# Two layers of cached attention and an MLP on one core: half a MB of the first wq and half a MB of the last w2 moved to partitions 0 to 31

## The chip, the core and the metric

The kernel runs on one core of a Trainium2 chip. TensorE (PE in the profile, with its weight loads as PEld) multiplies, VectorE (DVE), ScalarE (ACT) and GpSimd (POOL) do the rest, and SyncE (SP) issues nearly all the DMAs. The core has 16 DMA engines, which move data from HBM into SBUF, a memory of 128 partitions. The metric is the device time of one execution in microseconds (us), as the median of several runs.

## The reference

One token of each of 8 sequences passes through two identical layers, with the same weights both times. All data are float32.

```
B, D = 8, 1024;  Hq, Hkv, Sk, Dh = 32, 4, 4096, 128;  F = 3584
for layer in range(2):
    x = x + attention(layernorm(x) @ wq, k_cache, v_cache) @ wo
    x = x + gelu(layernorm(x) @ w1 + b1) @ w2 + b2
```

Here wq is 1024 x 4096 and wo 4096 x 1024 (16 MB each), w1 is 1024 x 3584 and w2 3584 x 1024 (14 MB each), and each of the 8 sequences has 8 MB of keys and 8 MB of values. One layer reads some 188 MB; the second layer finds a little of the cache still in SBUF.

## The kernel before, in words

**The arena.** One SBUF tile, `arena`, holds all that is streamed. It has 216 units of 256 columns (1 KB in each partition, so 128 KB in a unit). Three large slots A, B and C begin at units 0, 64 and 128, and four small ring slots R of 8 units at 184, 192, 200 and 208. Small intermediates have places of their own in the ring's units: the spread-out queries (`AT_QZ`, 3 units), a row of scores (`AT_ROW` or `AT_ROW2`, 4 units) and the turned probabilities (`AT_S`, 4 units).

**The stream.** `weights` and `cache` (lines 414 to 432) write one list, `stream`, with every load of both layers in the order in which it will be used: a name, a place and the piece of DRAM. `pump` (line 160) takes loads from its head while their places are free, and issues each as one DMA on SP's queue. `give` frees a place and pumps again, so a load is issued when the work that read the old contents is through. Since SP issues in order, a load that waits holds all the later ones back. The large loads are issued long before they are used; the ring of 8 unit slots, which carries wo, w1, w2 and wq between the two layers, runs four loads ahead.

**The rows of a load.** A load writes 128 rows, one in each partition: 64 KB each for a load of 8 MB, 4 KB each for one of 512 KB.

**The products.** `expand` (line 174) multiplies the normalised row by wq or w1, in two halves u of 8 contraction blocks; with wq, one half is 8 MB. `project` (line 262) multiplies by wo or w2 and adds to the row: each contraction block of 128 rows is 4 units (512 KB), and takes four matmuls that write four groups of 32 output partitions. The first `expand` waits for the input row, the first half of wq, and then the second half. The last `project`, `p1`, reads w2 in six pieces of 40, 28, 20, 12, 8 and 4 units; after it come one addition on VectorE and the store of the result.

**Attention.** For each sequence `scores` multiplies the queries by the keys, `probs` and `turn` make and transpose the probabilities, `values` multiplies by the values, and `heads` scales the result. In layer 0 the order of the loads is K0, V0 up to K7, V7, then wo (`o0`). The first three pieces of `o0` have free ring slots before the attention ends; the fourth goes where `AT_S` lies, and waits until the last values are through.

**Small loads.** The bias b2 is loaded by four DMAs of 8 rows of 1 KB (line 475), queued behind K0, and b1 by one DMA of 128 rows of 112 bytes behind them.

Of the kernel before, what the change touches and what calls it, by code (L numbers as in the profile page):

```python
# [8 lines left out]
F32 = mybir.dt.float32  # L9
# [5 lines left out]
P = 128  # L15
B, D = 8, 1024
# [20 lines left out]
SLOT = 64  # L37
AT_A, AT_B, AT_C, RING = 0, 64, 128, 184
N_KB = 216
AT_QZ, AT_ROW, AT_S, AT_ROW2 = 200, 208, 212, 203  # L40
Q_AT = (0, 48, 72, 32)
QW = 88
DMA_SCRATCH = 512
# [3 lines left out]
def decode_layers(ctx: ExitStack, tc: tile.TileContext, x, kc, vc, wq, wo, w1, b1, w2, b2, out):  # L47
# [82 lines left out]
    def layernorm(xr, rsum):  # L130
# [23 lines left out]
        pending.append(variance)  # L154
        return rs

    stream = []
    held = {}

    def pump():  # L160
        while stream and is_free(stream[0][1], stream[0][2]):
            key, at, n, src = stream.pop(0)
            take(at, n, key)
            nc.sync.dma_start(out=arena[:, at * KB:at * KB + src.shape[1]], in_=src)
            held[key] = at, n

    def loads(name):
        i = 0
# [2 lines left out]
            yield i, at, n  # L171
            i += 1

    def expand(name, unit, rs, finish, hooks={}):
        heights = [(unit // P - j + 3) // 4 * P for j in range(4)]
        for u in range(2):
            acc = ps_o.tile([P, CH], F32, tag="o", name="acc")
            at = 0
            begun = set()
            end = NT * unit  # L180
            for i, base, n_kb in loads((name, u)):
                c = given = 0
                cols = min(n_kb * KB, end - at)
                while c < cols:
                    kt, a = divmod(at, unit)
                    n = min(unit - a, cols - c)
                    blocks = arena[:, base * KB + c:base * KB + c + n].rearrange("p (t q) -> p t q", q=P)
                    t0, t1 = a // P, (a + n) // P
                    for j in range(4):
                        ts = range(t0 + (j - t0) % 4, t1, 4)  # L190
                        if len(ts):
                            r = ts[0] // 4
                            nc.tensor.matmul(acc[32 * j:32 * j + 32, r * P:(r + len(ts)) * P],  # L193
                                             xnT[:, kt * B:kt * B + 32],
                                             blocks[:, ts[0] - t0:ts[-1] - t0 + 1:4],
                                             start=(j not in begun), stop=(kt == NT - 1 and ts[-1] + 4 >= unit // P))
                            begun.add(j)
# [64 lines left out]
    def project(name, n_k, lhs, rsum, hooks={}):  # L262
        y = ps_o.tile([P, CH], F32, tag="o", name="y")
        kt = 0
        step = D // KB
        for i, base, n_kb in loads(name):
            for c in range(0, n_kb, step):
                for j in range(4):
                    e = (base + c) * KB + j * Q4
                    nc.tensor.matmul(y[32 * j:32 * j + 32, 0:Q4], lhs[:, kt * B:kt * B + 32], arena[:, e:e + Q4],  # L270
                                     start=(kt == 0), stop=(kt == n_k - 1))
                kt += 1
                if kt in hooks:
                    hooks[kt]()
                if c + step == n_kb:
                    give(base, n_kb)
                if kt >= 4:
                    flush()
        assert kt == n_k
        nc.vector.scalar_tensor_tensor(x_row, y[:, 0:Q4], 1.0, x_row, op0=ALU.mult, op1=ALU.add, accum_out=rsum)  # L280
# [133 lines left out]
    def weights(name, dram, parts):  # L414

        for u in range(dram.shape[0]):
            a = 0
            for i, (at, n) in enumerate(parts[u]):
                cols = min(n * KB, dram.shape[2] - a)
                stream.append((((name, u) if dram.shape[0] > 1 else name, i), at, n, dram[u, :, a:a + cols]))  # L420
                a += cols
            assert a == dram.shape[2]

    def cache(layer, keys, dram, parts):

# [76 lines left out]
    for layer in range(2):  # L502
        pieces.update({key: at for (e, key), at in places.items() if e == layer})
        rs = layernorm(x_row, rsum)
        if layer == 0:
            expand("q0", W, rs, query_unit)
            flush()
            last = attention(range(B), kept, after={6: park})
        else:
# [10 lines left out]
        project(f"p{layer}", NFT, hT, rsum)  # L520

    nc.sync.dma_start(out=out, in_=x_row)

# [52 lines left out]
```

## Time and profile before

| | |
|---|---|
| time, median of 3 runs | 872.83 us (872.7 to 873.04) |
| the profiled execution | 873.06 us, span 871.1 us |
| TensorE busy | 535.9 us, 62% of the span, 4056 matmul instructions and as many weight loads |
| VectorE, ScalarE busy | 181.9 us and 47.5 us |
| HBM read | 369.28 MB, 424 GB/s over the span |
| queue q1 (SP's loads) | 17056 packets, 99.1% of the time of 16 DMA engines |
| queue q8 (blocks of TensorE's instructions) | 31 packets of 16 KB, 0.2% |

The span is what the profile sees of an execution; the execution's own time is 1.96 us longer. The profile has no column for a single DMA engine. It gives the share of time in which the 16 were busy, and for a stretch of time the number of packets of each queue. A packet here is one row of a load (or the 4 byte write that reports a load's end on one engine). The packed trace behind the profile holds each packet's start, length, size and queue, but not the engine it ran on.

### The profile page before, as it was taken

The page shows a single profiled execution, that of the slowest core. Times are in us where ns is not written, and L with a number is a line of the kernel's source. Part 1 is how long each engine was busy: PE and PEld are TensorE (multiplying, and loading weights), DVE is VectorE, ACT ScalarE, POOL GpSimd, SP SyncE. Part 2 cuts the span into 40 slices and gives each one's busy share as a digit, 9 for nine tenths or more (in the row PEclk, how much of TensorE's full clock was granted, in tenths as well). Part 3 has the DMA queues.
Part 4 walks back from the last instruction along what each step waited for, and adds up shares of the span by engine and source line. Part 5 has one row for each costly group of instructions (what it writes and reads, how often), then busy time and mean ns, then how long its engine had stood idle before and what let it go on. Part 6 is the DMA issues. An engine that isn't in the chain of part 4 may idle for free.

```text
span 871.1 us, 9135 instructions
## 1 busy us (share of the span) xinstructions
PE 535.9 (62%) x4056; PEld 179.3 (21%) x4056; DVE 181.9 (21%) x587; ACT 47.5 (5%) x75; POOL 2.6 (0%) x14
## 2 busy tenths in 40 slices
PE   0547566655667566776667766766565655665565
PEld 0112121211212122222222122222121211222222
DVE  0001221313122232200100034332232313120110
ACT  0200000000000010000000010000000000000000
POOL 0000000000000000000000000000000000000000
PEclk9877777877777778868876799987787777777889
DMA  9999999999999999999999999999999999999997
GB/s 390 434 433 434 434 431 434 433 431 434 436 428 434 436 412 428 400 420 420 421 421 418 418 426 438 440 431 431 433 431 431 433 434 433 432 433 440 419 423 296
DMA packets 17239, 369.99 MB, mean 425 GB/s; under 512 B 2064, under 2 KB 2352, under 8 KB 3504
## 3 DMA queue, kind: packets, MB, share of 16 engines
q1 hardware_dynamic: 17056, 369.28, 99.1%
q8 instruction: 31, 0.51, 0.2%
q10 hardware_dynamic: 144, 0.13, 0.0%
q14 instruction: 8, 0.07, 0.0%
HBM read 369.28 MB, written 0.13 MB: 424 GB/s over the span
## 4 chain that ended last, share of the span: by engine, by line
DMA 72%; PE 21%; DVE 5%; issue 1%; ACT 1%; SPq 0%; ACTq 0%; DVEq 0%
DMA arena<-in_A_v_cache_dram 27%; DMA arena<-in_B_w_dram 17%; DMA arena<-in_A_k_cache_dram 16%; PE sps L303 6%; PE o_ps L360 6%; DMA arena<-in_A_wo_dram 6%; DMA arena<-in_A_wq_dram 4%; PE acc L193 3%; DVE scratch L368 3%; DMA x_row<-in_A_x_dram 3%; PE y L270 2%; PE sps L375 1%; DVE scratch L366 1%; PE s_ps L303 1%; DVE arena L311 1%
## 5 line engine op out<-in xcount | busy, mean ns | idle before, releaser
L303 PE MATMUL sps<-arena 128*32 128x512 f32 x944 | 135.4, 712 | 90.3 <-DMA arena<-in_A_k_cache_dram 78.1
L360 PE MATMUL o_ps<-arena 128*32 128x512 f32 x1024 | 154.7, 732 | 8.4 <-DMA arena<-in_A_v_cache_dram 8.3
L270 PE MATMUL y<-arena,oT 128*32 128x256 f32 x960 | 79.3, 476 | 50.3 <-DMA arena<-in_A_wo_dram 28.5
L193 PE MATMUL acc<-arena,xnT 128*32 128x512 f32 (+3 forms) x608 | 78.5, 618 | 47.7 <-DMA arena<-in_B_w_dram 27.2
L368 DVE SCALAR_TENSOR_TENSOR scratch<-o_ps,misc,scratch 128x128 f32<-128x128 f32 x192 | 67.3, 351 | 6.8
L303 PEld LDWEIGHTS sps<-arena 128*32 128x32 f32 x944 | 30.0, 125 | 173.2 <-DMA arena<-in_A_k_cache_dram 77.0
L338 PE MATMUL sps<-ident,arena 128*128 128x128 f32 x128 | 30.2, 379 | 43.6 <-ACT arena L327 31.7
L270 PEld LDWEIGHTS y<-arena,oT 128*32 128x32 f32 x960 | 32.2, 130 | 97.5 <-DMA arena<-in_A_wo_dram 33.2
L375 PE MATMUL sps<-misc,scratch 128*128 128x8 f32 x128 | 27.5, 287 | 33.4 <-DVE scratch L368 33.4
L311 DVE TENSOR_SCALAR_CACHE_REDUCE arena<-sps 128x512 f32<-128x512 f32 x30 | 20.8, 692 | 121.6 <-PE sps L303 121.6
L327 ACT ACTIVATE arena<-arena,bias 128x1024 f32<-128x1024 f32 x16 | 18.4, 1148 | 506.4 <-DVE scratch L324 506.4
L360 PEld LDWEIGHTS o_ps<-arena 128*32 128x32 f32 x1024 | 30.9, 127 | 69.5 <-issue 58.3
L375 PEld LDWEIGHTS sps<-misc,scratch 128*128 128x128 f32 x128 | 21.6, 212 | 104.9 <-DVE scratch L368 85.7
L366 DVE TENSOR_SCALAR scratch<-o_ps,misc 128x128 f32<-128x128 f32 x64 | 22.5, 351 | 95.8 <-PE o_ps L360 95.8
L193 PEld LDWEIGHTS acc<-arena,xnT 128*32 128x32 f32 x608 | 20.4, 122 | 93.1 <-DMA arena<-in_A_wq_dram 36.8
L377 DVE TENSOR_TENSOR oT<-sps,scratch 128x8 f32<-128x8 f32 x64 | 11.1, 173 | 113.6 <-PE sps L375 113.6
L338 PEld LDWEIGHTS sps<-ident,arena 128*128 128x128 f32 x128 | 19.2, 186 | 52.1 <-ACT arena L327 35.5
L280 DVE SCALAR_TENSOR_TENSOR x_row<-y,x_row 128x256 f32<-128x256 f32 x4 | 1.7, 424 | 104.8 <-PE y L270 104.8
L320 PE MATMUL sps<-scratch,misc 128*128 128x128 f32 x32 | 7.8, 326 | 18.7 <-DVE scratch L316 18.7
L343 DVE COPY arena<-sps 128x512 f32<-128x512 f32 x16 | 11.1, 692 | 38.5 <-PE sps L338 38.5
L345 PE MATMUL sps<-scratch,misc 128*128 128x32 f32 x32 | 10.0, 404 | 12.5 <-DVE arena L343 12.5
L132 PE MATMUL sps<-nmean,rsum 128*128 128x64 f32 x8 | 2.0, 336 | 25.3 <-DVE rsum L473 23.6
(74 smaller groups left out, 134.5 us busy)
## 6 DMA issues: line engine op xcount, KB each, us to landing
arena<-in_B_w_dram SPq DMA_DIRECT2D x27, 1024.0 KB, 8.6
arena<-in_A_wo_dram SPq DMA_DIRECT2D x15, 1024.0 KB, 8.0
arena<-in_A_wq_dram SPq DMA_DIRECT2D x15, 1024.0 KB, 8.3
arena<-in_B_w_dram SPq DMA_DIRECT2D x2, 7168.0 KB, 45.2
arena<-in_A_k_cache_dram SPq DMA_DIRECT2D x3, 4096.0 KB, 19.5
arena<-in_A_v_cache_dram SPq DMA_DIRECT2D x3, 4096.0 KB, 22.5
arena<-in_A_v_cache_dram SPq DMA_DIRECT2D x4, 2048.0 KB, 18.2
arena<-in_B_w_dram SPq DMA_DIRECT2D x1, 5120.0 KB
```

What stands on the lines that cost most here:

```text
L193: nc.tensor.matmul(acc[32 * j:32 * j + 32, r * P:(r + len(ts)) * P], xnT[:, kt * B:kt * B + 32], blocks[:, ts[0] - t0:ts[-1] - t0 + 1:4], ...
L270: nc.tensor.matmul(y[32 * j:32 * j + 32, 0:Q4], lhs[:, kt * B:kt * B + 32], arena[:, e:e + Q4], start=(kt == 0), stop=(kt == n_k - 1))
L303: nc.tensor.matmul(ps[32 * g:32 * g + 32, :], q[:, c:c + 32], kt[:, g * CH:(g + 1) * CH], start=(j == 0), stop=(j == HKV - 1))
L311: nc.vector.tensor_scalar(row[:, half * CH:(half + 1) * CH], ps, SCALE, None, op0=ALU.mult, op1=ALU.max, accum_out=st["mx"][:, half:half + 1])
L327: nc.scalar.activation(row, row, AF.Exp, bias=bias, scale=1.0, accum_out=ls)
L338: nc.tensor.transpose(pp[:, t * P:(t + 1) * P], row[:, c:c + P], ident)
L343: nc.vector.tensor_copy(s[:, half], src)
L360: nc.tensor.matmul(o[32 * g:32 * g + 32, :], s[:, g], v[:, g * CH:(g + 1) * CH], start=(half == 0), stop=(half == NH - 1))
L366: nc.vector.tensor_scalar(r, o[:, 0:P], sel_t[:, 0:1], None, op0=ALU.mult)
L368: nc.vector.scalar_tensor_tensor(r, o[:, t * P:(t + 1) * P], sel_t[:, t:t + 1], r, op0=ALU.mult, op1=ALU.add)
L375: nc.tensor.matmul(po[:, 0:REP], scratch[:, a:a + DH], sel_h, start=True, stop=True)
L377: nc.vector.tensor_tensor(oT_v[:, j * REP:(j + 1) * REP, b], po[:, 0:REP], scratch[:, a + j * REP:a + (j + 1) * REP], ALU.mult)
```

## The change

Two pieces of 512 KB leave the loads of 128 rows. One is the last contraction block of the second half of the first wq (128 rows of 1024 columns), the other the last contraction block of w2 in the second layer. Each is now laid on partitions 0 to 31, as four groups of 32 rows side by side, so 16 KB in each of 32 partitions, in units 192 to 207 of the arena. Four DMAs load it; DMA m takes the rows m, m+4, up to m+28 of each group, that is 8 partitions with four runs of 4 KB each.

A product over such a piece needs the left operand's rows 32 to 127 moved to partitions 0 to 31 as well: `low_lhs` does that with three small matmuls against slices of the identity and one copy into a new tile `low`. The block's four matmuls then become sixteen, over 32 rows each.

To make room, `AT_QZ`, `AT_S` and `AT_ROW2` change places and the third and fourth ring slots change order. The pieces of the last w2 become 44, 28, 20, 12 and 4 units.

```
-AT_QZ, AT_ROW, AT_S, AT_ROW2 = 200, 208, 212, 203
+AT_QZ, AT_ROW, AT_S, AT_ROW2 = 212, 208, 200, 204
+LOW, AT_LOW = 32, 192
+NLOW = P // LOW
...
+    low = const.tile([LOW, (NLOW - 1) * B + PAD], F32, name="low")
+    nc.gpsimd.memset(low, 0.0)
+
+    def low_load(dram, name):
+        stream.append((name, AT_LOW, 16, dram))
+
+    def low_lhs(src):
+        pl = small_ps("pt")
+        for g in range(1, NLOW):
+            nc.tensor.matmul(pl[0:LOW, (g - 1) * B:g * B], ident[:, g * LOW:(g + 1) * LOW], src[:, 0:B], start=True, stop=True)
+        nc.vector.tensor_copy(low[:, 0:(NLOW - 1) * B], pl[0:LOW, 0:(NLOW - 1) * B])
+        return [src[0:LOW, 0:32]] + [low[:, g * B:g * B + 32] for g in range(NLOW - 1)]
...
+            if isinstance(key, str):
+                src = src.rearrange("(g p) c -> p g c", g=NLOW)
+                dst = place(at, n)[0:LOW].rearrange("p (g c) -> p g c", g=NLOW)
+                for m in range(4):
+                    nc.sync.dma_start(out=dst[m:LOW:4], in_=src[m:LOW:4])
+                continue
...
+                    if extra and u == 1 and at == 0:
+                        part = low_lhs(xnT[:, (NT - 1) * B:NT * B + PAD])
+                        t = low_tile(extra)
+                        for g in range(NLOW):
+                            products((unit - D) // P, t[:, g].rearrange("p (t q) -> p t q", q=P), part[g], range(end // P))
+                        give(AT_LOW, 16)
...
+                if extra and kt == n_k // 2:
+                    part = low_lhs(lhs[:, n_k * B:n_k * B + 32])
+                    t = low_tile(extra)
+                    for g in range(NLOW):
+                        for j in range(4):
+                            nc.tensor.matmul(y[32 * j:32 * j + 32, 0:Q4], part[g], t[:, g, j * Q4:(j + 1) * Q4], start=False, stop=False)
+                    give(AT_LOW, 16)
...
-    R = [RING + 8 * i for i in range(4)]
+    R = [RING, RING + 8, RING + 24, RING + 16]
...
-    weights("q0", wq, [[(A, SLOT)], [(Bb, SLOT)]])
+    lows = ("q0", "p1")
+    weights("q0", wq, [[(A, SLOT)], [(Bb, SLOT - 4)]])
+    stream.insert(1, stream.pop())
...
-    weights("p1", w2, [[(A, 40), (A + 40, 28), (A + 68, 20), (A + 88, 12), (A + 100, 8), (A + 108, 4)]])
+    weights("p1", w2, [[(A, 44), (A + 44, 28), (A + 72, 20), (A + 92, 12), (A + 104, 4)]])
+    stream.insert(-5, stream.pop())
```

On SP's queue at the start of the program, this is the order of the loads before (wq's two halves, K0, b2, b1, V0, K1):

```order
L164 DMA arena<-in_A_wq_dram 128x16384 x2
L164 DMA arena<-in_A_k_cache_dram 128x16384
L475 DMA b_row<-in_B_b_dram 8x256 x4
L476 DMA misc<-in_B_b_dram 128x28
L164 DMA arena<-in_A_v_cache_dram 128x16384
```

And this is the order now (lines 188 and 190 are both in `pump`):

```order
L190 DMA arena<-in_A_wq_dram 128x16384
L188 DMA arena<-in_A_wq_dram 8x4x1024 x4
L190 DMA arena<-in_A_wq_dram 128x15360
L190 DMA arena<-in_A_k_cache_dram 128x16384
L524 DMA b_row<-in_B_b_dram 8x256 x4
L525 DMA misc<-in_B_b_dram 128x28
L190 DMA arena<-in_A_v_cache_dram 128x16384
```

The four DMAs of 8 partitions stand between the two halves of wq, and the second half's rows are 60 KB instead of 64 KB. At the end of SP's queue stood the two halves of w1, six pieces of w2 and the store:

```order
L164 DMA arena<-in_B_w_dram 128x14336 x2
L164 DMA arena<-in_B_w_dram 128x10240
L164 DMA arena<-in_B_w_dram 128x7168
L164 DMA arena<-in_B_w_dram 128x5120
L164 DMA arena<-in_B_w_dram 128x3072
L164 DMA arena<-in_B_w_dram 128x2048
L164 DMA arena<-in_B_w_dram 128x1024
L522 DMA out_dram<-x_row 128x256
```

Now these stand there:

```order
L190 DMA arena<-in_B_w_dram 128x14336 x2
L188 DMA arena<-in_B_w_dram 8x4x1024 x4
L190 DMA arena<-in_B_w_dram 128x11264
L190 DMA arena<-in_B_w_dram 128x7168
L190 DMA arena<-in_B_w_dram 128x5120
L190 DMA arena<-in_B_w_dram 128x3072
L190 DMA arena<-in_B_w_dram 128x1024
L574 DMA out_dram<-x_row 128x256
```

The four new DMAs stand ahead of all pieces of w2, and the piece of 8 units (rows of 2048 columns) is gone. On TensorE, the last `project` now reads as follows, where line 305 is the usual product, 168 `low_lhs`, and 315 the product over the moved block:

```order
L305 MATMUL y<-arena,oT 32x256 x16
L256 MATMUL sps<-ident,scratch 128x128 x3
L256 MATMUL sps<-ident,scratch 128x64
L305 MATMUL y<-arena,oT 32x256 x36
L168 MATMUL sps<-oT,ident 32x8 x3
L315 MATMUL y<-arena,oT 32x256 x4
L315 MATMUL y<-arena,low 32x256 x12
L305 MATMUL y<-arena,oT 32x256 x56
```

Before, 112 matmuls of line 270 stood there with the four transposes of line 221 among them; now there are 108, and 3 and 16 in their middle.

More of the change, by code (lines that the diff above doesn't have):

```diff
@@ L180, in expand, with products @@
             end = NT * unit
+            def products(begin, blocks, lhs, rest):
+                for j in range(4):
+                    ts = range(begin + (j - begin) % 4, begin + blocks.shape[1], 4)
+                    if len(ts):
+                        r = ts[0] // 4
+                        nc.tensor.matmul(acc[32 * j:32 * j + 32, r * P:(r + len(ts)) * P], lhs,
+                                         blocks[:, ts[0] - begin:ts[-1] - begin + 1:4], start=(j not in begun),
+                                         stop=not any(e % (unit // P) % 4 == j for e in rest))
+                        begun.add(j)
+            if extra and u == 1:
+                end -= D
             for i, base, n_kb in loads((name, u)):
@@ L187, in expand @@
                     blocks = arena[:, base * KB + c:base * KB + c + n].rearrange("p (t q) -> p t q", q=P)
[L188 to L197, printed above, removed]
+                    products(a // P, blocks, xnT[:, kt * B:kt * B + 32], range((at + n) // P, end // P))
+                    if extra and u == 1 and at == 0:
[4 more added lines that the diff above has]
+                        give(AT_LOW, 16)
                     c += n
@@ L421, in weights @@
                 a += cols
-            assert a == dram.shape[2]
+            if name in lows and u == dram.shape[0] - 1:
+                assert a == dram.shape[2] - D
+                low_load(dram[u, :, a:a + D], name + "low")
+            else:
+                assert a == dram.shape[2]
     def cache(layer, keys, dram, parts):
@@ L505, in decode_layers @@
         if layer == 0:
-            expand("q0", W, rs, query_unit)
+            expand("q0", W, rs, query_unit, extra="q0low")
             flush()
@@ L519, in decode_layers @@
         rsum = row_sums()
-        project(f"p{layer}", NFT, hT, rsum)
+        if layer == 0:
+            project("p0", NFT, hT, rsum)
+        else:
+            project("p1", NFT - 1, hT, rsum, extra="p1low")
     nc.sync.dma_start(out=out, in_=x_row)
```

10 lines of the change are left out of this document (7 added, 3 removed).

## The prediction

> **What bounds the kernel now.** The page comes first. In it I read the busy share of the DMA engines in 40 slices (tenths, 9 is 90% or more), the queues, and the chain that ended last.
>
> ```profile
> span 871.1 us, 9135 instructions
> ...
> PE 535.9 (62%) x4056; PEld 179.3 (21%) x4056; DVE 181.9 (21%) x587; ACT 47.5 (5%) x75; POOL 2.6 (0%) x14
> ...
> DMA  9999999999999999999999999999999999999997
> ...
> q1 hardware_dynamic: 17056, 369.28, 99.1%
> q8 instruction: 31, 0.51, 0.2%
> ...
> DMA 72%; PE 21%; DVE 5%; issue 1%; ACT 1%; SPq 0%; ACTq 0%; DVEq 0%
> ```
>
> The loads fill 99.1% of the time of 16 DMA engines, so the engines' own work sets the time, and TensorE, busy for 62%, only follows. What is left to ask is whether all 16 end together. The chain's last pieces (start, length, what) and the windows of the last 8 us (each row: length, busy time of the engines, clock, and as the last two numbers the DMA share and GB/s) say no:
>
> ```profile
> 824.68 42.46 DMA arena<-in_B_w_dram
> 867.15 0.04 issue
> 867.19 0.68 PE y L270 x8
> 867.88 0.02 issue
> 867.90 0.42 DVE x_row L280
> ```
>
> ```profile
> 859.00:862.00 3.00, 2.19 (x40) 1.20 (x40) 0.00 (x0) 0.00 (x0) 0.00 (x0) 1.00 1.00 418
> 862.00:863.70 1.70, 0.39 (x8) 0.16 (x8) 0.00 (x0) 0.00 (x0) 0.00 (x0) 1.00 0.62 260
> 863.70:865.10 1.40, 1.29 (x24) 0.52 (x16) 0.00 (x0) 0.00 (x0) 0.00 (x0) 1.00 0.55 228
> 865.10:866.10 1.00, 0.15 (x4) 0.16 (x8) 0.00 (x0) 0.00 (x0) 0.00 (x0) 1.00 0.45 184
> 866.10:866.60 0.50, 0.50 (x12) 0.26 (x9) 0.00 (x0) 0.00 (x0) 0.00 (x0) 1.00 0.19 74
> 866.60:867.10 0.50, 0.42 (x8) 0.00 (x0) 0.00 (x0) 0.00 (x0) 0.00 (x0) 1.00 0.00 0
> ```
>
> The last piece of w2 was issued at 824.68 and arrives at 867.15, so the issue is early and the queue is what it waits for. Around 862 the share falls to 0.55, which is 9 of 16 engines; two more stop at about 865, and the other seven at 866.1 to 866.7. Averaged over the 16, the idle time is 0.38 x 1.7 + 0.45 x 1.4 + 0.55 x 1.0 + 0.81 x 0.5 = 2.2 us. That is the most that an even spread could give.
>
> Why are some engines late? TensorE's instructions come by DMA too, 31 blocks of 16 KB. Two of them, in windows of 1.5 us (175.0 to 176.5) and 1.6 us (211.2 to 212.8):
>
> ```profile
> q8 instruction: 1, 0.02, 4.2%
> ```
>
> ```profile
> q8 instruction: 1, 0.02, 4.0%
> ```
>
> 4.2% of 16 engines over 1.5 us is 1.0 us of one engine. The views have no engine numbers, but on one engine a packet starts 3 to 4 ns before the one ahead of it ends, so the 17056 packets of q1 (row above) can be strung into 16 chains. I followed them from the first wq row to about 360 us, and again from about 421 us to the end. Each block stops one chain for 1.55 us in all, and the blocks go round the same eight chains in the same order, about four to each. Call these the fetch eight. At the end seven of them are the last (866.1 to 866.7); the eighth, with three blocks, and one more chain that carries another engine's code stop at 865.0 to 865.1.
>
> **Which engines get the new loads.** A load of 8 rows stands in the trace already, b2's four. The window from 60.6 to 63 us, around them:
>
> ```profile
> DMA packets 240, 1.10 MB, mean 457 GB/s; under 512 B 192, under 2 KB 224, under 8 KB 224
> ```
>
> 224 - 192 = 32 rows of 1 KB. Of the 192 small ones 128 are b1's rows and 64 are end reports: 16 each for K0 and b1, and 32 for b2, so 8 for each of its DMAs. A DMA of 8 rows thus runs on eight engines, one row on each. Between the end of K0 and the start of V0, eight chains take 280 ns and the other eight 87 to 104 ns, with nothing between; the eight slow ones are those with b2. Call them the row eight.
>
> Two chains are in both sets: they carry b2 rows, and take the blocks at 175.2 and 211.3 us (the two windows above). Six of the row eight fetch nothing for TensorE, and six of the fetch eight get no rows. Links at the two chains are unambiguous from b2 on to their blocks, but for one improbable exchange.
>
> **The change part by part.** Each piece of 512 KB puts 64 KB on each of the row eight and takes 32 KB from all 16. The prices are from windows in which all engines move long rows (62.5 on), 4 KB rows (392.8 on) and 8 KB rows (396 on):
>
> ```profile
> 62.50:120.00 57.50, 35.53 (x222) 11.27 (x222) 13.07 (x43) 3.68 (x6) 0.00 (x0) 0.77 1.01 435
> 392.80:395.50 2.70, 2.36 (x24) 0.95 (x24) 0.00 (x0) 0.00 (x0) 0.00 (x0) 0.60 1.02 411
> 396.00:460.00 64.00, 40.05 (x430) 15.01 (x422) 6.20 (x22) 4.02 (x7) 0.16 (x1) 0.82 1.01 421
> ```
>
> 64 KB in 4 KB rows takes 65.5 KB / (411/16 GB/s) = 2.55 us. In wq the 32 KB go from long rows: 32.8 KB / (435/16) = 1.21 us. In w2 a piece of 8 KB rows goes and another grows: 32.8 KB / (421/16) = 1.25 us. So each of the row eight gets 1.34 + 1.30 = 2.64 us of work, and each of the others loses 1.21 + 1.25 = 2.46 us.
>
> Work added early counts at the end only on an engine that never idles. There is one idle place, after the attention of layer 0, when the fourth piece of wo waits for the last values:
>
> ```profile
> 357.00:359.00 2.00, 1.22 (x14) 0.57 (x14) 1.16 (x4) 0.00 (x0) 0.00 (x0) 1.00 1.03 430
> 359.00:359.50 0.50, 0.50 (x12) 0.15 (x7) 0.00 (x0) 0.00 (x0) 0.00 (x0) 1.00 0.67 279
> 359.50:360.00 0.50, 0.50 (x16) 0.26 (x8) 0.40 (x2) 0.00 (x0) 0.00 (x0) 1.00 0.63 262
> 360.00:360.50 0.50, 0.36 (x8) 0.00 (x0) 0.46 (x2) 0.00 (x0) 0.00 (x0) 1.00 0.59 246
> ```
>
> Early engines idle there for up to 2 us; the two common chains, already late by a block, for 0.27 and 0.41 us. With 1.34 us more they don't idle at all. They ended at 866.34 and 866.42, so they now end at 866.34 + 2.64 - 0.27 = 868.71 and 866.42 + 2.64 - 0.41 = 868.65. The last engine before ended at 866.73: **the last load arrives 2.0 us later.** The fetching engines without rows move up, and nobody waits for them.
>
> After the last load there is the tail of TensorE (start, length, line, count in instruction pairs):
>
> ```profile
> 863.49 1.50 PE L270 MATMUL y<-arena,oT 128*32 128x256 f32 x24 [1.31 <-DMA arena<-in_B_w_dram]
> 865.95 1.07 PE L270 MATMUL y<-arena,oT 128*32 128x256 f32 x16 [0.96 <-DMA arena<-in_B_w_dram]
> 867.19 0.64 PE L270 MATMUL y<-arena,oT 128*32 128x256 f32 x8 [0.18 <-DMA arena<-in_B_w_dram]
> ```
>
> The piece ahead of the last is now 12 units, 24 instructions and 1.50 us instead of 1.07. It starts 1.24 us before the last piece is there (867.19 - 865.95) and ends 0.26 us after; the last block then follows back to back, at 0.53 us for a block, and ends at 0.79 instead of 0.64: **0.1 us.**
>
> The rest costs nothing. Seven more DMAs on SP take 0.3 to 0.5 us each, by b2's four, tens of us ahead of need (42.46 us for the last piece):
>
> ```profile
> L475 SPq DMA_DIRECT2D b_row<-in_B_b_dram x4: 282/308/475, 2.1 to 3.3; - x4
> ```
>
> If that cover were gone they would cost 7 x 0.3 = 2.2 us. The 30 more matmuls fall into stretches in which PE waits for loads (1.3 and 0.96 us ahead of the blocks above); without the wait the 15 of each place, 30 instructions where 8 take 0.53 us, would cost 2 us. The exchange of ring places lets the third piece of wo go only after `turn` of the last sequence, whose last step is this one:
>
> ```profile
> 346.70 0.36 DVE L347 RECIPROCAL scratch<-sps 128x32 f32<-128x32 f32 x1 [0.73 <-PE sps L345]
> ```
>
> The engines are full until 359, so it is issued in time, with nothing behind it but the fourth piece, which waits longer anyway.
>
> Sum against the profiled execution: 871.1 + 2.0 + 0.1 = 873.2 us of span, and 873.06 + 2.1 = 875.1 us. The median shown lies 0.2 us under that execution, so **874.9 us**.
>
> Bounds: with 4 KB rows as cheap as long ones, the two pieces add 2.4 us in all and the sum is 1.9 us; with no credit for idle time 2.5 us. The 30 matmuls are 120 instructions of TensorE (each is two matmul instructions with a weight load) beside 2 x 4056, so a 32nd block may come; on one of the common chains it adds 1.55 us (876.4).
>
> [...] The trace has a block hold one engine for 1.0 us and delay its chain by 1.55. [...]
>
> **The rivals.**
>
> *The DMAs use 16 engines.* b2 has one run per row, the new loads four, so it is unproved that they are split alike. With 32 runs over 16 engines nothing is rebalanced: 32 KB at 2.55/2 = 1.28 us instead of 1.21 or 1.25, twice, and the tail, 0.2 us: 873.0 us. This decides at the first four DMAs: eight or 16 end reports. Not slower. 0.08.
>
> *Rows and blocks are on complementary engines.* My chains would have to be crossed at both common ones. The fetch eight gain, and the ninth late chain, which ended at 865.0 with rows of its own, ends at 865.0 + 2.64 - 0.3 = 867.3: 0.6 us later than 866.7, 873.4 us. Against it: both chains have their b2 rows by 280 ns. 0.07.
>
> *As that, and the ninth has no rows.* Then all late engines lose work, 1.25 us in w2, and in wq what is not given back at 359 us: 871.6 us, at best 870.4. 0.07, half of it past 0.2%.
>
> *Fixed cost.* [...] 0.01.
>
> **How the numbers follow.** The forecast has 0.74, and 0.03 goes to a 32nd block on a common chain. I call 0.2%, 1.75 us, the bound between same and another time. The forecast's 2.1 us is close to it: I give 0.58 of its 0.74 to slower. Slower: 0.58 + 0.03 + 0.01 = 0.62. Same: 0.16 + 0.08 + 0.07 + 0.03 = 0.34. Faster: 0.04. The range, 873.0 to 875.7, takes in the forecast with its bounds and the first two rivals.
>
> **What would show it.** In the changed profile the first engines should stop at about 861 (those without rows and blocks), most of them by 865.5, and a share of 2/16 should stand alone from about 867.3 to 868.7; the matmuls after the last load should end near 869.9. At the start, 4 DMAs of 8 rows should leave 32 end reports. A share that falls in one step would mean an even spread, and a last load before 867 would make the prediction wrong.

## The result, and the profile after

| | before | after |
|---|---|---|
| time, median of 11 runs each | 872.82 us (872.5 to 874.14) | 875.1 us (874.89 to 875.83) |
| ratio, 95% interval | | 1.0025 (1.0017 to 1.0033) |
| the profiled execution | 873.06 us, span 871.1 us | 875.1 us, span 873.3 us |
| blocks of TensorE's code | 31 | 32 |

The change costs 2.3 us by the medians and 2.2 us by the spans. First the page of the changed kernel, its span, the engines' busy times, the DMA packets by size and the queues:

```profile
span 873.3 us, 9296 instructions
...
PE 548.3 (63%) x4124; PEld 184.4 (21%) x4124; DVE 182.3 (21%) x589; ACT 47.5 (5%) x75; POOL 2.7 (0%) x15
...
DMA packets 17416, 370.01 MB, mean 424 GB/s; under 512 B 2112, under 2 KB 2400, under 8 KB 3808
...
q1 hardware_dynamic: 17232, 369.28, 98.9%
q8 instruction: 32, 0.52, 0.2%
```

The bytes of q1 are the same (369.28 MB), and so is nearly the share. The loads as a whole have not become slower; what has changed is when each engine ends. The row of packets in the page of before lets the end reports be counted:

```profile
DMA packets 17239, 369.99 MB, mean 425 GB/s; under 512 B 2064, under 2 KB 2352, under 8 KB 3504
```

There are 48 more packets under 512 B. The last w2 has one load of 128 rows fewer (16 reports fewer), so the eight new DMAs left 48 + 16 = 64, eight each: each of them ran on eight engines.

The windows of the end (length, busy time of the engines, clock, and as the last two numbers the DMA share and GB/s):

```profile
861.00:863.00 2.00, 2.00 (x40) 1.00 (x36) 0.00 (x0) 0.00 (x0) 0.00 (x0) 1.00 0.89 375
863.00:865.00 2.00, 1.34 (x28) 0.58 (x24) 0.00 (x0) 0.00 (x0) 0.00 (x0) 1.00 0.69 279
865.00:866.00 1.00, 1.00 (x24) 0.62 (x20) 0.00 (x0) 0.00 (x0) 0.00 (x0) 1.00 0.24 102
866.00:867.00 1.00, 0.88 (x18) 0.26 (x8) 0.00 (x0) 0.00 (x0) 0.00 (x0) 1.00 0.23 94
867.00:868.00 1.00, 0.00 (x0) 0.00 (x0) 0.00 (x0) 0.00 (x0) 0.00 (x0) 1.00 0.12 49
868.00:868.50 0.50, 0.35 (x8) 0.26 (x12) 0.00 (x0) 0.00 (x0) 0.00 (x0) 1.00 0.14 57
868.50:869.00 0.50, 0.50 (x16) 0.28 (x12) 0.00 (x0) 0.00 (x0) 0.00 (x0) 1.00 0.04 16
```

The share is under 0.9 from 861 on. Between 865 and 867 it is 0.24, about 4 engines of 16. From 867 to 868.5 it is 0.12 to 0.14, which is 2 of 16, and these two carry the last rows alone. From 867 to 868 TensorE does nothing but wait for them. Its timeline at the end (start, length, engine and line, count in instruction pairs, in brackets the idle time ahead and what ended it):

```profile
864.51 2.37 PE L305 MATMUL y<-arena,oT 128*32 128x256 f32 x40 [0.66 <-DMA arena<-in_B_w_dram]
868.15 1.93 PE L305 MATMUL y<-arena,oT 128*32 128x256 f32 x32 [1.28 <-DMA arena<-in_B_w_dram]
869.39 0.21 PEld L305 LDWEIGHTS y<-arena,oT 128*32 128x32 f32 x8 [0.22 <-DMA arena<-in_B_w_dram]
870.15 0.42 DVE L322 SCALAR_TENSOR_TENSOR x_row<-y,x_row 128x256 f32<-128x256 f32 x1 [10.25 <-PE y L305]
```

The last matmuls end at 868.15 + 1.93 = 870.08; before, it was 867.19 + 0.64 = 867.83. The whole 2.25 us lies between these two ends. The weight load at 869.39 is the first work that the last piece releases; before, that was at 867.19.

The packet records tell more of the two engines. Strung into 16 chains by start and length from 770 us on, as in the prediction, the last two chains end at 868.65 and 868.87. Each of them carries 16 rows of the new load of w2, and each pauses for 1.0 us beside a block of TensorE's code (the blocks at 808.6 and 827.5 us). The third last, at 867.42, carries 16 rows and has no such pause; the fourth, at 866.44, has a pause and none of the rows. All others end by 865.3.

### The profile page after: what moved, and what is told of

The parts are those of the page before. It is cut to its first block, busy times and chain, and to the rows that moved or that the text cites. A ratio compares the mean times of both kernels' runs of the same rounds, so it can differ in the third digit from the quotient of the medians.

```text
span 873.3 us, 9296 instructions
## 1 busy us (share of the span) xinstructions
PE 548.3 (63%) x4124; PEld 184.4 (21%) x4124; DVE 182.3 (21%) x589; ACT 47.5 (5%) x75; POOL 2.7 (0%) x15
## 2 busy tenths in 40 slices
DMA packets 17416, 370.01 MB, mean 424 GB/s; under 512 B 2112, under 2 KB 2400, under 8 KB 3808
## 3 DMA queue, kind: packets, MB, share of 16 engines
q1 hardware_dynamic: 17232, 369.28, 98.9%
HBM read 369.28 MB, written 0.13 MB: 423 GB/s over the span
## 4 chain that ended last, share of the span: by engine, by line
DMA 69%; PE 22%; DVE 7%; ACT 1%; issue 1%; ACTq 0%; SPq 0%; DVEq 0%
DMA arena<-in_A_v_cache_dram 22%; DMA arena<-in_B_w_dram 16%; DMA arena<-in_A_k_cache_dram 15%; DMA arena<-in_A_wo_dram 9%; PE o_ps L402 7%; PE sps L345 7%; DMA arena<-in_A_wq_dram 4%; DVE scratch L410 4%; DMA x_row<-in_A_x_dram 3%; PE acc L211 2%; PE y L305 2%; PE sps L417 2%; DVE scratch L408 1%; PE sps L380 1%; DVE arena L353 1%
## 5 line engine op out<-in xcount | busy, mean ns | idle before, releaser
L211 PE MATMUL acc<-arena,xnT 128*32 128x512 f32 (+3 forms) x616 | 81.6, 633 | 48.5 <-DMA arena<-in_B_w_dram 26.2
```

## The experiments

The theory is the forecast's: the time is set by the engines that carry both rows of the new loads and code for TensorE. The first two experiments test the other ways of cutting the load, the next ones each piece alone, then come fewer engines for one piece, and last the two kinds of work, code and rows, each without the change.

### The same pieces by DMAs of 16 rows

```
-                for m in range(4):
-                    nc.sync.dma_start(out=dst[m:LOW:4], in_=src[m:LOW:4])
+                for m in range(2):
+                    nc.sync.dma_start(out=dst[m:LOW:2], in_=src[m:LOW:2])
```

> The same two pieces on partitions 0 to 31, but each loaded by two DMAs of 16 rows instead of four of 8, so that all 16 DMA engines should carry 32 KB of each. All other parts of the change stay (places, extra matmuls, the pieces of w2 of 44, 28, 20, 12 and 4 units). Theory (uneven load of the 16 engines): nothing is rebalanced; 2 x 0.05 us for the shorter rows and 0.1 us for the tail on TensorE: 873.0 us, 0.2 above the kernel before, and the DMA share at the end falls as it did before. Rival (the cost is the extra matmuls, the changed places or the shorter last pieces, not the engines): 875.1 us, as in the changed kernel.

Measured: 878.64 us (877.69 to 878.9), ratio 1.0062 (1.0049 to 1.0074). That is 5.8 us slower than before, and both theories miss. An even spread over 16 engines should have cost nothing, and the spread is even: the page has 2112 packets under 512 B, as many as the changed kernel, so 64 end reports for four DMAs. The window over the load of the first piece, in the changed kernel and then in this one:

```profile
15.00:35.00 20.00, 10.91 (x86) 3.85 (x86) 1.27 (x5) 4.71 (x6) 0.00 (x0) 1.00 0.96 414
```

```profile
15.00:35.00 20.00, 10.29 (x86) 3.73 (x86) 1.05 (x5) 4.71 (x6) 0.00 (x0) 1.00 1.00 396
```

The DMA engines are busier (1.00 for 0.96) and move less (396 for 414 GB/s), so it is the single packets that take longer. In the records, half of the 4 KB rows of the first piece take 0.31 us or more, where every one of them takes 0.159 us in the changed kernel. Rows of 64 KB at that time take up to 3.5 us instead of 2.42; during the second piece it is up to 4.6 us per 64 KB. At the same bytes a DMA now has 16 rows and 16 engines instead of 8 and 8, and its partitions lie 2 apart and not 4; this run doesn't show which of these makes the rows slow. The next one keeps the 8 rows and engines of a DMA.

### The same pieces by DMAs of 8 neighbouring rows

The bytes are those of the change, and so is the number of engines (2112 packets under 512 B here too, so eight for each DMA). What differs is the partitions of each DMA, and with them the rows of the weight that it reads.

```
-                    nc.sync.dma_start(out=dst[m:LOW:4], in_=src[m:LOW:4])
+                    nc.sync.dma_start(out=dst[8 * m:8 * m + 8], in_=src[8 * m:8 * m + 8])
```

> The change with one thing altered: DMA m takes the partitions 8m to 8m+7 instead of m, m+4 up to m+28. Rows, bytes, engines and matmuls stay. [...] Rival (the 16-row run was slow for another reason, say the number of rows of a DMA): 875.1 us, as with the stride.

Measured: 885.74 us (885.28 to 886.69), ratio 1.0148 (1.0134 to 1.0161). The same window:

```profile
15.00:35.00 20.00, 10.35 (x86) 3.86 (x86) 0.97 (x4) 4.71 (x6) 0.00 (x0) 1.00 0.98 322
```

322 GB/s for 414 at nearly the same share (0.98 for 0.96). The 4 KB rows of the first piece take up to 0.59 us, and the 64 KB rows beside them up to 5.9 us. The same bytes on as many engines cost 10.4 us more with neighbouring rows than with the stride of 4 (12.7 against 2.3, each against the kernel before in its own comparison). I had put the time at 888 to 890 us, by an estimate whose terms no run shows; the direction came as expected, the loss 2 to 4 us smaller. The number of rows of a DMA, the rival's cause, is 8 in both. Whether the wait is on the writing or on the reading side is not shown: each DMA reads the rows of the weight that belong to its partitions, so with the partitions the order of the rows read from HBM changes as well, and no run changes one without the other.

### One piece alone

The first experiment keeps only the piece of wq, the second only that of w2:

```
-    lows = ("q0", "p1")
+    lows = ("q0",)
```

> Only the piece of the first wq is moved; the last w2 is loaded and multiplied as before. Theory: the two engines with both loads get 1.34 us ahead of the idle place after layer 0's attention, lose 0.27 and 0.41 us of idle time there, and end at 866.34 + 1.34 - 0.27 = 867.41 where the last one ended at 866.73: +0.7 us, 873.5 us. Rival (whatever is added ahead of the idle place is lost in it): 872.8 us. Second rival (both pieces cost the same half of 2.3 us): 873.95 us.

Measured: 873.95 us (873.65 to 875.49), ratio 1.0009 (1.0001 to 1.0018).

```profile
866.92 1.07 PE L305 MATMUL y<-arena,oT 128*32 128x256 f32 x16 [0.97 <-DMA arena<-in_B_w_dram]
868.15 0.64 PE L305 MATMUL y<-arena,oT 128*32 128x256 f32 x8 [0.16 <-DMA arena<-in_B_w_dram]
```

The last piece comes at 868.15 instead of 867.19, +0.96 us, and the median lies 1.1 us over that of before (872.85). The theory's 873.5 is under all eleven runs, so it missed, and the second rival's 873.95 is the measured time to the digit. But the trace shows neither cause. These are the stretches from 360 to 363 us, before and then here:

```profile
360.00:363.00 3.00, 1.75 (x26) 0.71 (x18) 1.18 (x4) 0.00 (x0) 0.00 (x0) 1.00 0.93 333
```

```profile
360.00:363.00 3.00, 2.54 (x41) 0.98 (x33) 1.40 (x4) 0.00 (x0) 0.00 (x0) 1.00 0.60 197
```

All 16 engines together idle (0.93 - 0.60) x 3.0 = 1.0 us longer on average at the place after layer 0's attention, where the fourth piece of wo waits for TensorE's last values; these start at 359.58 instead of 358.43. That is the whole delay. At the end many engines are late and not two: the share is 0.54 from 866 to 867. So this run doesn't measure what wq's rows cost on the two engines. Why the values start later here, when in the changed kernel they start earlier (357.70), no run shows.

```
-    lows = ("q0", "p1")
+    lows = ("p1",)
```

> Only the piece of the last w2 is moved, the first wq is loaded as before. Theory: the two engines with both loads end at 866.42 + 1.30 = 867.72 instead of 866.73, and the tail adds 0.1 us: +1.1 us, 873.9 us. At the end 2 of 16 engines are busy alone from about 866.3 to 867.7. Rival (the end has no part in it, the first piece delays everything): 872.9 us.

Measured: 873.79 us (873.57 to 875.25), ratio 1.0013 (1.0004 to 1.0022).

```profile
867.10 1.93 PE L305 MATMUL y<-arena,oT 128*32 128x256 f32 x32 [1.31 <-DMA arena<-in_B_w_dram]
```

The matmuls end at 867.10 + 1.93 = 869.03, +1.20 us, and the median lies 0.94 us over that of before: near the theory's 1.1, and clear of the rival's 872.9. The share at the end is less sharp than expected:

```profile
866.00:867.00 1.00, 0.00 (x0) 0.00 (x0) 0.00 (x0) 0.00 (x0) 0.00 (x0) 1.00 0.19 70
```

That is three engines, and from 867 to 868 it is 0.05, less than one, where two to the end were expected. The two pieces together give 0.96 + 1.20 = 2.16 us, and the change 2.25, but as the first delay comes from another place, that they add up is luck. These ends are those of one execution each, and the times of the kernel before run from 872.43 to 874.27 us, so a few tenths between two of them say nothing.

### The last piece by fewer engines

The second kernel above (w2's piece alone), once with eight DMAs of 4 rows at a stride of 8, and once on 16 partitions with four DMAs of 4 rows at a stride of 4.

```
-                for m in range(4):
-                    nc.sync.dma_start(out=dst[m:LOW:4], in_=src[m:LOW:4])
+                for m in range(8):
+                    nc.sync.dma_start(out=dst[m:LOW:8], in_=src[m:LOW:8])
```

> As the kernel with the last piece only, but loaded by eight DMAs of 4 rows, so that four engines carry 128 KB each (5.1 us) and all 16 lose 1.25 us. Theory: each of the four ends 3.85 us later than before, the others 1.25 us earlier. If neither of the two engines with both loads nor the ninth late one is among the four, the four end at 865.8 to 867.1, the rest by 865.5: 872.0 to 873.3 us. If one of the two is among them, 866.42 + 3.85 = 870.3: 876.5 us; if only the ninth late one is, 865.0 + 3.85 = 868.9: 875.1 us. Rival (the load of a few rows costs by the number of its DMAs, now eight): slower than the kernel with the last piece in four DMAs by about as much as that one is than the kernel before, 875.0 us, with all 16 engines ending as in that one.

Measured: 877.26 us (875.95 to 877.52), ratio 1.0041 (1.0028 to 1.0055). Most 4 KB rows of the piece take 0.159 us; one in ten takes 0.31 us or more, up to 0.39, and 64 KB beside them take up to 4.3 us. But the loss is elsewhere. These are SP's loads of w2 in the kernel with four DMAs and in this one (start of the first issue, time until the last is through, line, count), and the stretch from 829 to 834 us in the same order:

```profile
805.17 28.67 SPq L190 DMA_DIRECT2D arena<-in_B_w_dram  x5
```

```profile
789.28 45.80 SPq L188 DMA_DIRECT2D arena<-in_B_w_dram  x8
835.19 2.54 SPq L190 DMA_DIRECT2D arena<-in_B_w_dram  x5
```

```profile
829.00:834.00 5.00, 0.98 (x8) 0.51 (x12) 0.00 (x0) 0.00 (x0) 0.00 (x0) 0.50 1.01 426
```

```profile
829.00:834.00 5.00, 0.00 (x0) 0.00 (x0) 0.00 (x0) 0.00 (x0) 0.00 (x0) 0.56 0.33 125
```

The last of the eight small DMAs is issued 45 us after the first, and the five pieces behind it only from 835.19 on, 30 us later than with four DMAs. The queue runs dry, and the engines idle for two thirds of these 5 us. So the run doesn't answer which engines are late, and a cost that comes with the number of DMAs, as the rival had it, isn't excluded. Why SP issues the last ones so late, no run here shows.

On 16 partitions the piece is eight groups of 16 rows, and its block takes 32 matmuls. Four engines carry 128 KB each, 5.1 us by twice the 2.55, and all 16 lose 1.25 us:

```
-LOW, AT_LOW = 32, 192
+LOW, AT_LOW = 16, 184
```

> [...] Theory (which engines carry it decides): if neither the two engines with both loads nor the ninth late one is among the four, these end at 861.9 to 863.2 + 3.85 = 865.8 to 867.05, all others by 866.73 - 1.25 = 865.5: 871.9 to 873.2 us, and the DMA share near the end stands at 4/16. If the ninth is among them, 865.0 + 3.85 = 868.85: 875.0 us. If one of the two is, 866.42 + 3.85 = 870.3: 876.5 us. Rival (any load of a few rows delays the end by its bytes per engine, whichever engine): more than 3.85 - 1.25 us late, 875.4 us or above.

Measured: 880.13 us (877.72 to 880.33), ratio 1.0077 (1.0063 to 1.0091), and a miss. The page has 2064 packets under 512 B, as before, with one load of 128 rows fewer (16 reports), so 16 end reports for the four DMAs, four engines each. The rows take 0.159 us, and the last of them starts at 868.51 in the profiled execution (877.72 us, the shortest of the five). Yet the kernel ends long after:

```profile
863.00:868.00 5.00, 5.00 (x48) 1.99 (x44) 0.00 (x0) 0.00 (x0) 0.00 (x0) 0.50 0.31 125
868.00:869.00 1.00, 1.00 (x16) 0.53 (x12) 0.00 (x0) 0.00 (x0) 0.00 (x0) 0.55 0.04 16
869.00:870.00 1.00, 1.00 (x28) 0.52 (x24) 0.00 (x0) 0.00 (x0) 0.00 (x0) 1.00 0.00 0
870.00:872.00 2.00, 2.00 (x44) 1.14 (x40) 0.00 (x0) 0.00 (x0) 0.00 (x0) 1.00 0.00 0
```

TensorE is busy without a pause from 863 on, at a granted clock of 0.50 until 868, while the loads are through before 869. Twice as many small matmuls for the piece (32 instead of 16, and 7 instead of 3 to turn the left operand) and the low clock have put TensorE behind the loads; how much each did isn't separated. The cover that hid 15 more matmuls at this place didn't hide 35. The DMA side reads as expected for the case in which the ninth late chain, but neither common one, is among these four engines (0.04 is less than one engine of 16, after 868). TensorE hides it in the time, so I tried it again without matmuls, below.

### More code for TensorE

The kernel before, with small matmuls that nobody reads; no load is changed. First 640 of them, all in layer 1:

```
+        if "dummy" in st:
+            for i in range(10):
+                nc.tensor.matmul(st["dummy"][0:32, 0:1], nmean, sel_x[:, 0:1], start=True, stop=True)
```

> The kernel before with 640 more tiny matmuls (one column each, into an unused bank) between the values of layer 1, 10 after each tile: no more data, some 2560 more instructions of TensorE, 10 more blocks of code. Each takes about 0.07 us, 45 us in all, in stretches where TensorE waits for loads. Theory (a block delays the engine that carries it by 1.55 us, and the blocks go round eight engines): each of the eight gets one more, two of them two; the last end moves by 1.5 us (9 more) to 2.6 us (10 more, both extra ones on an engine that was late): 874.3 to 875.5 us, with the other engines ending where they ended. Rival (the engines' spread has another cause, and blocks are hidden): 872.9 us.

Measured: 903.99 us (902.74 to 906.2), ratio 1.0358 (1.0342 to 1.0374). Inconclusive: the rows of the weight loads and of the matmuls, which overlap in part, show 79.9 and 74.8 us of new work for TensorE where 45 were expected. The share of q1 falls to 96.4%, so the loads now wait for TensorE.

```profile
L363 PEld LDWEIGHTS spot<-sel_x,nmean 128*32 128x32 f32 x1280 | 79.9, 153 | 80.2 <-issue 80.2
L363 PE MATMUL spot<-sel_x,nmean 128*32 128x1 f32 x1280 | 74.8, 190 | 0.0
```

Then 232 of them, one or two for each tile of the values in layer 0 and two or three in layer 1 (`n` is 1 and 2):

```
+        if "spare" in st:
+            for i in range(st["n"] + half):
+                nc.tensor.matmul(st["spare"][0:32, 0:1], nmean, sel_x[:, 0:1], start=True, stop=True)
```

> The kernel before with 232 more matmuls of one column on TensorE, one to three for each tile of the values (928 instructions, 58 KB of code, 3 or 4 more blocks); no load is changed. TensorE gets some 57 us of work spread over 112 tiles, by the run with 640 of them, and should still follow the loads. Theory: three or four of the fetch eight get one block more, 1.55 us each, stop alone at about 868.2 instead of 866.1 to 866.7, and the end moves by 1.5 us: 874.4. Rival (a block is hidden): 873.0.

Measured: 873.97 us (873.62 to 875.49), ratio 1.0009 (1.0000 to 1.0018).

```profile
q8 instruction: 35, 0.57, 0.3%
```

```profile
866.00:867.00 1.00, 0.36 (x8) 0.00 (x0) 0.00 (x0) 0.00 (x0) 0.00 (x0) 1.00 0.29 119
867.00:868.00 1.00, 0.89 (x16) 0.42 (x16) 0.00 (x0) 0.00 (x0) 0.00 (x0) 1.00 0.12 49
```

```profile
867.12 1.07 PE L270 MATMUL y<-arena,oT 128*32 128x256 f32 x16 [0.76 <-DMA arena<-in_B_w_dram]
868.36 0.64 PE L270 MATMUL y<-arena,oT 128*32 128x256 f32 x8 [0.17 <-DMA arena<-in_B_w_dram]
```

Four blocks more, and the last piece comes at 868.36 instead of 867.19, 1.17 us later. TensorE still waits for each of the last pieces, so it is the loads that are late, and no load has changed. Nor do the loads wait longer for TensorE's extra work: at the idle place after layer 0's attention, from 357 to 363 us, the share is 0.95 (374 GB/s), against 0.92 (355 GB/s) before. Strung into chains from 770 us on, the four that end last (867.1 to 867.9) each pause for 1.0 us or a little more beside one of the blocks from 804 us on. The rival (a block is hidden) gave 0, the theory 1.5; the missing 0.3 us is the size of the idle time after layer 0's attention, which a block ahead of it would use up (argued, not followed).

### More code for GpSimd

GpSimd is idle after its last memset (the page of before has 14 instructions and 2.6 us busy for it). 2048 more of them, of one column, add code and next to no work for the others:

```
+        for i in range(2048):
+            nc.gpsimd.memset(spare, 0.0)
```

> The kernel before with 2048 memsets of one column on the idle GpSimd behind its last work: 128 KB more code, about 8 blocks of 16 KB, and no load, no matmul changed. Theory (a block delays its DMA engine by 1.55 us, and the late engines are late by their blocks): if GpSimd's blocks go round the same eight engines, each gets one more and the end moves by 1.5 us, to about 874.4; if they go round the other eight, the end stays (873.0), with those engines stopping 1.55 us later than 862 to 863; if all went to one engine, the end moves by some 10 us. Rival (a block costs no engine more than its 16 KB, 0.6 us): at most +0.6 us, 873.5.

Measured: 879.09 us (878.79 to 879.65), ratio 1.0067 (1.0055 to 1.0080), +6.2 us.

```profile
q8 instruction: 31, 0.51, 0.2%
q14 instruction: 24, 0.20, 0.1%
```

```profile
867.00:868.00 1.00, 1.00 (x20) 0.38 (x12) 0.00 (x0) 0.00 (x0) 0.00 (x0) 1.00 0.09 37
868.00:873.00 5.00, 2.60 (x44) 1.09 (x40) 0.00 (x0) 0.00 (x0) 0.00 (x0) 1.00 0.05 22
```

```profile
873.04 0.64 PE L273 MATMUL y<-arena,oT 128*32 128x256 f32 x8 [0.17 <-DMA arena<-in_B_w_dram]
```

TensorE's queue q8 has its 31 blocks, and q14 has 24 instead of the 8 in this row of before:

```profile
q14 instruction: 8, 0.07, 0.0%
```

0.13 MB in 16 more blocks is 8 KB each; TensorE's are of 16 KB (0.51 MB in 31). The share of 0.05 from 868 to 873 is 0.8 of one engine of 16, which I read as one engine alone for 5 us. The last piece comes 873.04 - 867.19 = 5.85 us later. By this reading the third case of the expectation happened, at a smaller size (6.2 us instead of some 10). If it is the ninth late chain, which ended at 865.05 and carries another engine's code, it now ends at 866.73 + 5.85 = 872.6: 7.5 us for 16 blocks, 0.47 us each. If it is another engine that ended earlier, a block cost more. The 8 KB themselves take 0.31 us by their records. Code that nobody waits for moved the end of this kernel by 6.2 us, through the loads behind it.

### A load that nobody reads

The kernel before, with w2's piece loaded once more to partitions 0 to 31, ahead of the last five pieces; nothing is removed, and no matmul is added. `LOW` is 32:

```
+            if key == "dummy":
+                src = src.rearrange("(g p) c -> p g c", p=LOW)
+                dst = place(at, n)[0:LOW].rearrange("p (g c) -> p g c", c=D)
+                for m in range(4):
+                    nc.sync.dma_start(out=dst[m:LOW:4], in_=src[m:LOW:4])
+                continue
```

> The kernel before with one load more that nobody reads: 512 KB to partitions 0 to 31 by four DMAs of 8 rows, ahead of the last five pieces of w2; no matmul is added. Theory: 2.55 us more on each of the row eight; the two common engines end at 866.4 + 2.55 = 868.95 instead of the last at 866.7, +2.25 us: 875.2, with a share of 2/16 alone at the end. Rival (rows and blocks on complementary engines): the ninth late engine at 865.05 + 2.55 = 867.6, +0.9: 873.9. Rival (DMAs spread over 16 engines): +1.27: 874.2.

Measured: 874.98 us (874.61 to 875.78), ratio 1.0019 (1.0010 to 1.0028).

```profile
867.00:868.00 1.00, 0.12 (x4) 0.00 (x0) 0.00 (x0) 0.00 (x0) 0.00 (x0) 1.00 0.15 61
```

```profile
868.05 1.07 PE L277 MATMUL y<-arena,oT 128*32 128x256 f32 x16 [0.93 <-DMA arena<-in_B_w_dram]
869.29 0.64 PE L277 MATMUL y<-arena,oT 128*32 128x256 f32 x8 [0.17 <-DMA arena<-in_B_w_dram]
```

The last piece comes 2.10 us later (869.29 for 867.19), where the theory gave 2.25, an even spread 1.27 and complementary engines 0.9. It is the price of the 64 KB on an engine that is already among the last. The last three chains of packets (867.75, 868.49 and 868.77) carry 16 of these rows each, as in the change, as far as the links can be followed. The end of the change is here without its matmuls, its places and its 32nd block.

The same with `LOW` = 16: half the bytes, 64 KB on each of only four engines.

> The kernel before with one load more that nobody reads: 256 KB to partitions 0 to 15 by four DMAs of 4 rows, so 64 KB on each of four engines as in the load of 8 rows; no matmul is added, so TensorE's clock can't hide the engines' end as in the run with a block on 16 partitions. Theory after that run (the ninth late engine is among these four, the two common ones are not): one engine alone ends at 865.05 + 2.55 = 867.6, +0.9: 873.9. If a common engine were among the four: +2.25, 875.2. If none of the late engines were: no change, 873.0.

Measured: 874.26 us (873.47 to 875.43), ratio 1.0013 (1.0004 to 1.0022). The packets, and the end in the profiled execution (873.47 us, the shortest of the runs):

```profile
DMA packets 17319, 370.25 MB, mean 425 GB/s; under 512 B 2080, under 2 KB 2368, under 8 KB 3584
```

```profile
867.93 0.64 PE L277 MATMUL y<-arena,oT 128*32 128x256 f32 x8 [0.17 <-DMA arena<-in_B_w_dram]
```

2080 - 2064 = 16 end reports for four DMAs, so each ran on four engines. The last piece comes 0.74 us later, and the median 1.3: nearer to the 0.9 of one late engine among the four than to the 2.25 of a common one. The same 64 KB on an engine thus cost 2.1 us on eight engines and 0.7 on four by the profiled executions, 2.1 and 1.3 by the medians, whose intervals overlap. That it depends on which engines they fall on is the theory's reading; no record names the four.

## Why the prediction was right

The forecast, 874.9 us, lay 0.2 us under the median, and its mechanism is the one that the runs show. By the prediction's own bound of 0.2% the change is slower (2.3 us are 0.26%), though the interval reaches below that bound. That the time was met to 0.2 us is in part luck: executions of one kernel differ by more than that (872.5 to 874.14 us before), and two terms of the sum, wq's 1.34 us and the credit for idle time, are not shown by themselves.

- **Eight engines for each of the new DMAs.** Shown by the end reports (64 for eight). The rival of 16 engines falls by that count. Its price, 873.0, falls too: spread over 16 engines these pieces took 878.6. I had passed over which partitions a DMA takes: at the stride of 4 a row takes 0.159 us, with 16 rows at a stride of 2 half of them take 0.31 or more, and 8 neighbouring rows take up to 0.59.
- **1.34 us for the piece of wq, 1.30 for that of w2.** The piece of w2 alone should cost 0.99 us and 0.1 of tail; it measured 0.94 by the medians and 1.20 by the profiled executions. The piece of wq alone should move the last load by 0.68 us (866.34 + 1.34 - 0.27 = 867.41, against 866.73); the kernel took 1.1 us longer by the medians, but its trace shows a longer wait of all the engines after layer 0's attention, and so the 1.34 us aren't tested.
- **Two engines in both sets.** The share of 2/16 stands alone from 867 to 868.5, as the forecast said, and the two chains that end last carry rows and a block each. The third last, with rows and no block of TensorE's, ends at 867.42, where the ninth late chain should end by the same kind of sum (865.0 + 2.64 - 0.3 = 867.3). The load that nobody reads, on eight engines, costs 2.1 us without any other part of the change; four blocks of code cost 1.2 us without any load. Rows and code delay the same end, and complementary engines, the second rival, would give 0.9 for that load. Which of the 16 engines these are, by number, the records don't say.
- **Level engines.** Another reckoning, blocks that cost the DMA engines nothing and eight engines with rows 2.6 us late, gives 872.8 + 2.6 = 875.4 us, which is as near to the measured time. It falls by the windows: two engines end last, and not eight. It falls as well by the four blocks that moved the end without any load.
- **The idle place after layer 0's attention.** Here the window of before, then that of after:

```profile
359.50:361.00 1.50, 1.24 (x24) 0.55 (x20) 1.32 (x4) 0.00 (x0) 0.00 (x0) 1.00 0.87 268
```

```profile
359.50:361.00 1.50, 0.31 (x8) 0.16 (x8) 0.77 (x3) 0.00 (x0) 0.00 (x0) 1.00 0.87 322
```

  268 GB/s become 322 in the same stretch. The place has moved, too: TensorE's last values start 0.73 us earlier (357.70 for 358.43). So this says only that engines still idle there, not which; the credit of 0.27 and 0.41 us is not tested by itself. The kernel with wq's piece alone shows that this wait can grow by 1.0 us from one kernel to the next, which the prediction had as fixed.
- **The tail.** The last piece releases TensorE at 869.39 instead of 867.19, 2.20 us later, where the forecast had 2.0. From there the matmuls end in 0.69 us (870.08 - 869.39), against 0.64 before: the tail grew by 0.05 us, where the forecast had 0.79 us and 0.1 more.
- **A 32nd block** came. It did no harm that can be seen: it starts at 864.61 us, after the pauses of the two last chains, and the load that nobody reads has 31 blocks and the same end to 0.2 us.
- **Covered work.** There are 34 more matmuls, where the prediction counted 30: the page has 68 more matmul instructions (4124 for 4056), two to a matmul. They and the DMA issues left no trace at the end: TensorE waits 1.28 us ahead of its last group. How thin that cover was is shown by the run on 16 partitions, with 35 more at the second place instead of 15.
- **A fixed cost of each DMA**, the last rival with its 0.01: no run shows such a term. The eight DMAs of 8 rows cost 2.3 us in all, and by the share of q1 (98.9%, 99.1% before) the engines don't stop for them.

No version tried beats the kernel before. The 2.2 us that its engines stand idle at the end are the most that any cut could give, and the loads of 8 rows tried here reach the engines that are last.

## What to carry to other kernels

Where the DMA engines are full (98.9% here), look at the end of each of them and not at the mean: here bytes moved to engines that look free cost most of their price (2.1 of 2.55 us), because some of these engines carry TensorE's code as well. Count the end reports of a DMA to see how many engines carry it (64 for eight DMAs here), and watch GB/s against the share: with neighbouring rows a share of 0.98 at 322 GB/s meant rows of up to 0.59 us instead of 0.159, and with eight DMAs of 4 rows a share of 0.33 meant engines with nothing to do. Instructions of an idle engine weren't free in this kernel: 2048 of them on GpSimd cost 6.2 us, since their code comes by DMA like the loads (0.13 MB more on q14). And look for a delay all along the stream before it is put down to the change: the kernel with wq's piece alone lost its time 500 us ahead of the end.

## What was not expected of the hardware

- **Which partitions and rows a small DMA takes made 10.4 us of difference on the same number of engines.** 512 KB twice on partitions 0 to 31 cost 2.3 us with 8 rows at a stride of 4, 5.8 us with 16 rows at a stride of 2 and 12.7 us with 8 neighbouring rows (885.74 against 873.01 of before in that comparison). Long rows that ran beside them took longer as well, as much as 5.9 us for 64 KB instead of 2.42.
- **GpSimd's code set the end of the run with its memsets.** By the share at the end (0.05 of 16 from 868 to 873) its 16 more blocks of 8 KB fell on one engine, at 0.47 us each or more by the estimate above, where TensorE's 31 blocks of 16 KB go round eight chains in the records of before. 2048 instructions of 99 ns on an idle GpSimd cost 6.2 us:

```profile
L247 POOL MEMSET spare<- 128x1 f32 x2048 | 201.7, 99 | 118.3
```

- **TensorE's granted clock** stood at 0.50 from 863 to 868 us in the run on 16 partitions, where it was 1.00 at that place in the changed kernel (rows above). Why, no run here shows.
